# Another order of all queues, and another split of copies, casts, scalings and products among four engines, in a one-core attention and SoLU kernel

## The chip, the cores and the metric

The kernel runs on one core of one Trainium2 chip. A core has a matrix engine (PE, with its weight loads shown apart as PEld), a vector engine (DVE), an activation engine (ACT), a general engine (POOL), and a sync engine (SP) whose queue issues nearly all DMAs here. Each engine works through its own queue in order, and the queues wait for each other by semaphores. The metric is the device time of one execution in microseconds (us); lower is better.

## The reference

Clustered attention over 4 batches, 8 heads, 768 positions and head size 64, then a two-layer block with a softmax-gated activation (SoLU) and a normalisation, over 3072 tokens, 512 model features and 1024 hidden features:

```python
q_assign = np.argmax(np.einsum('bhsd,hcd->bhsc', q_n, c_n), axis=-1)
k_assign = np.argmax(np.einsum('bhsd,hcd->bhsc', k_n, c_n), axis=-1)
mask = q_assign[:, :, :, None] == k_assign[:, :, None, :]
scores = scale * np.matmul(q, k.transpose(0, 1, 3, 2))
scores = np.where(mask, scores, -1000000000.0)
attn = softmax(scores)
x = np.matmul(attn, v)            # heads side by side: (3072, 512)
h = x @ w_in
solu = h * softmax(h)
ln = (solu - mean(solu)) / np.sqrt(var(solu) + 1e-06) * g_ln
out = ln @ w_out
```

The softmax and mean lines are shortened here; they run along the last axis.

## The kernel before, in words

Every step is a small function that is registered under a name with its engine and with the names it must follow. A dictionary `AWAY` gives the engine of those steps that do not run on their usual one. A list `ORDER` names every step once; `run()` walks it and issues each step, so the list fixes the order of each engine's queue. Between queues only the data decide.

The names, with the lines that the profile shows:

- `ld`, `lv`, `lo`, `li`, `lc`, `lg`: loads of q and k, v, w_out, w_in, centroids and the norm's scale (SP's queue, two of them on ACT's). `tx`, `tu`: DMA transposes of attention output and of u. `ou`: output.
- Start of batch 0, pair of heads by pair: `tp` transposes q and k on PE (L396) into a PSUM bank, `xa`/`xt` copy the two halves out (L407 on ACT, L409 on DVE). From batch 1 on `xt` is one DVE transpose (L421). A pair's `ca` casts fill the operands `qbig` and `kbig` (L437 on ACT, L439 and L441 otherwise).
- `cz`, `cp`, `cb`: the centroids are normalised on DVE (L925 last), transposed on PE (L931) and spread on DVE (L934). `cl` multiplies with the centroids (L470). `tb`, `mx`, `oh`, `ot` turn that into one-hot rows on DVE (L479, L489, L493, L505 or L500). `pl` copies these below q and k (L529 on ACT, L531 otherwise), so that one product gives scores and mask. `bl` clears a part (L543).
- `S`: scores, 144 regions of 1024 columns in two halves `.0` and `.1` (L641). `E`: exponential of one region on ACT (L651). `V`: product with v (L663), v cast by `cv` (L554 on ACT, L556 otherwise). `N`: division by the sums on DVE (L675, L686). The scores use two PSUM tiles in turn: S of region n waits for E of region n-2.
- Tiles of 128 tokens, f = 0 to 23: `h` first product (L774), `hm` copy with running minimum on DVE (L784), `ex` exponential on ACT (L800), `u` the product h times e (L807, DVE or POOL), `bn`, `as`, `ag`, `al` the statistics (L818, L837, L823 and L825, L842), `y` second product (L846), `sc` scaling of the result (L859 on ACT, L861 on DVE).
- `me`, `mk`, `mf`, `km`, `ce`: w_out is centred once (L602, L611, L614, L618 or L622 and L624). `wi` casts w_in (L580). For the last two tiles u is transposed on PE (`ptu`, L761) and kept by `tu` (L768 DVE, L770 ACT).

Of the kernel before, what the change touches and what calls it, by code (L numbers as in the profile page):

```python
# [39 lines left out]
ld0.3.1 lg lv0.2 lo1 lo2 lo0 cx z5 cy cz wu tp0.0.0.0 tp0.0.0.1 tp0.0.1.0 tp0.0.1.1 cp xa0.0.0  # L40
xt0.0.0 xa0.0.1 xt0.0.1 tp0.1.0.0 xa0.1.0 cb cl0.0 tb0.0 mx0.0 oh0.0 ot0.0 ca0.0.0.0.0 z3
ca0.0.1.0.0 ca0.0.0.0.1 cc ca0.0.0.1.1 ca0.0.0.1.0 pl0.0.1.1 pl0.0.0.0 ca0.0.1.0.1 ca0.0.1.1.1
ca0.0.1.1.0 tp0.1.0.1 tp0.1.1.0 xt0.1.0 xa0.1.1 cl0.0.1 tp0.1.1.1 cv0.0.1 xt0.1.1 pl0.0.0.1
tp0.2.0.0 tp0.2.0.1 tb0.0.1 mx0.0.1 oh0.0.1 ot0.0.1 pl0.0.1.0.1 pl0.0.1.0.0 pl0.0.1.1.1 cl0.1 sg
pl0.0.1.1.0 z1 ca0.1.1.0 cv0.0.0 ca0.1.0.0 xa0.2.0 pl0.0.1.0 tp0.2.1.0 xt0.2.0 xa0.2.1 S0.0 S0.1
E0 tp0.2.1.1 xt0.2.1 S1.0 tp0.3.0.0 S1.1 S2.0 S2.1 tp0.3.0.1 tb0.1 mx0.1 oh0.1 xa0.3.0 E1 E2 cl0.2
xt0.3.0 S3.0 S3.1 V0.0 V0.1 V1.0 S4.0 S4.1 V1.1 tp0.3.1.0 tb0.2 E3 S5.0 S5.1 E4 E5 ot0.1 N0 mx0.2
gt tp0.3.1.1 S6.0 S6.1 V2.0 V2.1 S7.0 S7.1 V3.0 V3.1 xa0.3.1 gk xt0.3.1 cl0.3 E6 E7 cv0.1.0
pl0.1.1.1 ca0.1.0.1 ca0.3.0.0 pl0.1.1.0 ca0.3.0.1 z2 ca0.1.1.1 oh0.2 pl0.1.0.0 pl0.1.0.1 gw S8.0
S8.1 S9.0 S9.1 me0 me1 ot0.2 tb0.3 pl0.2.1.0 N1 pl0.2.0.0 mx0.3 mk oh0.3 ca0.2.0.0 ca0.2.1.0  # L50
ca0.3.1.0 ca0.2.1.1 pl0.2.1.1 pl0.2.0.1 E8 E9 ca0.2.0.1 S10.0 S10.1 S11.0 S11.1 V4.0 V4.1 V5.0
V5.1 E10 S12.0 S12.1 cv0.2.1 E11 E12 mf N2 ot0.3 pl0.3.0.0 ld1.0.0.0 li0 ld1.0.0.1 ld1.0.0.2
ld1.0.0 ld1.0.1.0 lv0.3 ld1.0.1.1 ld1.0.1.2 ld1.0.1 cv0.1.1 ca0.3.1.1 pl0.3.1.0 pl0.3.0.1 cv0.2.0
cv0.3.0 cv0.3.1 wi0 S13.0 S13.1 V6.0 V6.1 S14.0 S14.1 V7.0 V7.1 pl0.3.1.1 N3 km ce0 E13 E14 S15.0
S15.1 S16.0 S16.1 E15 E16 V8.0 V8.1 S17.0 S17.1 E17 V9.0 V9.1 S18.0 S18.1 E18 S19.0 S19.1 N4 ce5
V10.0 V10.1 V11.0 V11.1 S20.0 S20.1 E19 S21.0 S21.1 E20 E21 li1 li3 N5 V12.0 V12.1 ptx0 S22.0
S22.1 V13.0 V13.1 li2 xt1.0.0 xt1.0.1 tx0 xt1.1.0 xt1.1.1 ld1.2.0.0 ld1.2.0.1 ld1.2.0.2 ld1.2.0
ld1.2.1.0 ld1.2.1.1 ld1.2.1.2 ld1.2.1 S23.0 S23.1 cl1.0 E22 E23 S24.0 S24.1 E24 S25.0 S25.1 E25
ca1.0.0.1 cl1.1 N6 tb1.0 tb1.1 mx1.0 ce6 ce1 ca1.0.1.0 wi1 wi3 wi2 z4 ca1.1.0.0 ca1.0.1.1
ca1.1.1.0 ca1.0.0.0 S26.0 V14.0 V14.1 S26.1 S27.0 V15.0 S27.1 V15.1 h0.0.0 h0.0.1 N7 E26 E27 S28.0  # L60
S28.1 E28 V16.0 V16.1 V17.0 S29.0 S29.1 h0.1.0 V17.1 S30.0 S30.1 E29 E30 oh1.0 hm0.0 N8 ot1.0 ce2
pl1.0.1.0 pl1.0.0.1 pl1.0.1.1 bl1.0 ce3 lv1.0 tx2 lv1.1 lv1.2 ld2.0.0.0 ld2.0.0.1 ld2.0.0.2 h0.1.1
S31.0 S31.1 V18.0 V18.1 V19.0 S32.0 S32.1 V19.1 h1.0.0 N9 hm0.1 pl1.0.0.0 xt1.2.0 E31 S33.0 S33.1
E32 E33 h1.0.1 S34.0 S34.1 V20.0 V20.1 V21.0 S35.0 S35.1 V21.1 h1.1.0 E34 E35 S36.0 S36.1 N10
hm1.0 xt1.2.1 h1.1.1 S37.0 S37.1 V22.0 V22.1 V23.0 E36 E37 S38.0 S38.1 E38 V23.1 cl1.2 N11 tb1.2
ce4 hm1.1 ex0.0 cv1.0.0 cv1.0.1 u0.0 ca1.1.0.1 S39.0 S39.1 S40.0 S40.1 V24.0 V24.1 h2.0.0 h2.0.1
V25.0 xt1.3.0 E39 E40 ex1.0 h2.1.0 h2.1.1 S41.0 S41.1 S42.0 hm2.0 h3.0.0 S42.1 V25.1 xt1.3.1 hm2.1
V26.0 V26.1 h3.0.1 E41 cl1.3 S43.0 as0 bn0.0 N12 tb1.3 mx1.2 oh1.2 bn0.1 E42 S43.1 S44.0 S44.1
V27.0 ex2.0 E43 E44 V27.1 h3.1.0 h3.1.1 V28.0 S45.0 S45.1 S46.0 S46.1 V28.1 V29.0 E45 E46 tu0
V29.1 y0.0 S47.0 S47.1 y0.1 N13 cv1.1.0 ca1.2.0.0 u1.0 ca1.2.1.0 ca1.1.1.1 cv1.1.1 ca1.3.0.1 as1  # L70
ca1.2.0.1 bn1.0 hm3.0 ot1.2 ce7 S48.0 S48.1 y0.2 V30.0 E47 E48 S49.0 S49.1 E49 tx4 ld2.0.0
ld2.0.1.0 tu1 ld2.0.1.1 ld2.0.1.2 ld2.0.1 lv1.3 ld2.2.0.0 ld2.2.0.1 ld2.2.0.2 V30.1 V31.0 V31.1
S50.0 S50.1 h4.0.0 S51.0 S51.1 E50 E51 V32.0 V32.1 y0.3 S52.0 S52.1 bn1.1 hm3.1 ag0 N14 pl1.2.0.0
pl1.2.0.1 pl1.2.1.1 pl1.2.1.0 h4.0.1 as2 bl1.2 hm4.0 ag1 al0 u2.0 ca1.2.1.1 S53.0 S53.1 V33.0
V33.1 h4.1.0 xt2.0.0 sc0 h4.1.1 hm4.1 bn2.0 bn2.1 E52 E53 ex3.0 V34.0 S54.0 S54.1 S55.0 S55.1 E54
V34.1 V35.0 h5.0.0 h5.0.1 S56.0 S56.1 y1.0 E55 S57.0 S57.1 E56 cv1.2.0 V35.1 E57 y1.1 hm5.0 N15
tu2 ou0 ld2.2.0 ld2.2.1.0 ld2.2.1.1 y1.2 S58.0 S58.1 E58 h5.1.0 S59.0 S59.1 V36.0 V36.1 V37.0
V37.1 V38.0 S60.0 S60.1 h5.1.1 E59 E60 ex4.0 V38.1 y1.3 S61.0 S61.1 S62.0 S62.1 E61 E62 xt2.0.1
xt2.1.0 u3.0 ca2.0.0.1 ca2.0.0.0 al1 ag2 xt2.1.1 hm5.1 bn3.0 N16 bn3.1 cl2.1 cl2.0 tb2.1 ca1.3.1.0
cv1.2.1 ca1.3.0.0 as3 ag3 tb2.0 cv1.3.0 ca1.3.1.1 al2 u4.0 ca2.0.1.1 al3 ca2.1.0.0 ca2.1.1.0  # L80
cv1.3.1 V39.0 V39.1 S63.0 S63.1 S64.0 S64.1 V40.0 V40.1 sc1 V41.0 V41.1 y2.0 mx2.0 as4 N17 E63
S65.0 S65.1 E64 E65 y2.1 S66.0 S66.1 y2.2 y2.3 E66 tu3 tu4 ou1 ld2.2.1.2 ld2.2.1 S67.0 S67.1 V42.0
V42.1 S68.0 S68.1 V43.0 V43.1 sc2 oh2.0 ot2.0 N18 pl2.0.1.1 pl2.0.0.0 bn4.0 xt2.2.0 pl2.0.0.1
pl2.0.1.0 ca2.0.1.0 y3.0 E67 S69.0 S69.1 y3.1 ca2.2.0.1 bl2.0 E68 E69 S70.0 S70.1 E70 y3.2 V44.0
y3.3 V44.1 V45.0 S71.0 S71.1 S72.0 S72.1 V45.1 sc3 N19 tx6 y4.0 y4.1 E71 E72 S73.0 S73.1 E73 V46.0
V46.1 S74.0 S74.1 E74 y4.2 y4.3 V47.0 lv2.0 ou2 ld3.0.0.0 lv2.1 tx8 lv2.2 ex5.0 V47.1 S75.0 S75.1
E75 S76.0 h6.0.0 h6.0.1 S76.1 E76 bn4.1 xt2.2.1 ag4 xt2.3.0 N20 cv2.0.0 V48.0 V48.1 V49.0 h6.1.0
S77.0 S77.1 S78.0 S78.1 hm6.0 u5.0 bn5.0 V49.1 h6.1.1 hm6.1 V50.0 V50.1 cv2.0.1 xt2.3.1 N21
cv2.1.1 ca2.2.1.0 h7.0.0 h7.0.1 hm7.0 E77 E78 ca2.2.0.0 ca2.2.1.1 ca2.1.1.1 ca2.3.1.0 ex6.0 u6.0
cv2.1.0 ca2.3.0.0 al4 ca2.1.0.1 S79.0 S79.1 S80.0 S80.1 h7.1.0 E79 E80 V51.0 h7.1.1 V51.1 h8.0.0  # L90
S81.0 S81.1 h8.0.1 S82.0 S82.1 E81 E82 V52.0 V52.1 V53.0 V53.1 bn5.1 hm7.1 hm8.0 N22 cl2.3 cl2.2
tb2.3 tb2.2 mx2.2 sc4 oh2.2 ot2.2 pl2.2.0.0 S83.0 S83.1 S84.0 S84.1 V54.0 h8.1.0 h8.1.1 ex7.0 E83
S85.0 S85.1 E84 E85 pl2.2.0.1 pl2.2.1.1 V54.1 V55.0 V55.1 h9.0.0 ld3.0.0.1 ld3.0.0.2 tu5 S86.0
# [1267 lines left out]
```

## Time and profile before

| what | value |
|---|---|
| runs (us) | 222.46, 222.06, 220.9; median 222.06 |
| the profiled execution's own time | 221.02 us |
| its span, first to last instruction | 219.2 us |
| granted PE clock | 1.00 |
| DVE busy | 185.0 us (84%) |
| ACT busy | 193.0 us (88%) |
| POOL busy | 159.0 us (73%) |

A span of 219.2 us in an execution of 221.02 us leaves 1.8 us around it. "Busy" is the time in which at least one instruction of the engine is under way. A wait is put down to whatever ended it.

### The profile page before, as it was taken

Reading aid. Unit: us, or ns where it says so; the run is one execution under the profiler, and the core shown is the slowest. Engines: PE = TensorE matmul, PEld = TensorE weight load, DVE = VectorE, ACT = ScalarE, POOL = GpSimd, SP = SyncE. Lnnn points to the kernel's source line nnn. Section 1 sums busy time; section 2 is a strip of 40 time slices with the busy share of each in tenths; the row PEclk is TensorE's granted clock in tenths of the full one; section 3 lists DMA queues with packets and bytes.
Section 4 is the critical chain, followed back from the end, with each engine's and each line's share of the span. In section 5 each row is a group of like instructions: output and inputs, shape, how many; then the busy total and the mean of one; then the engine's idle time right before and its main releaser. Section 6 shows DMA issues by size and latency. Waiting matters only on the chain.

```text
span 219.2 us, 6308 instructions
## 1 busy us (share of the span) xinstructions
PE 211.8 (97%) x2429; PEld 148.0 (68%) x2429; DVE 185.0 (84%) x429; ACT 193.0 (88%) x246; POOL 159.0 (73%) x198
## 2 busy tenths in 40 slices
PE   7799999999999999999999999999999999999993
PEld 3467477677678776777677677666677766755552
DVE  3699978978999999896899999994888756889893
ACT  4699999999999998999999989999999888785472
POOL 4586969987898999549939987979969154555530
PEclk9999999999999999999999999999999999999999
DMA  6999999999799992998989973939484329695614
GB/s 198 372 403 299 180 182 301 150 155 274 134 189 175 164 185 45 174 250 174 190 211 173 180 155 63 178 96 215 133 162 101 93 48 171 138 151 132 185 60 156
DMA packets 120910, 38.33 MB, mean 175 GB/s; under 512 B 109992, under 2 KB 116400, under 8 KB 120880
## 3 DMA queue, kind: packets, MB, share of 16 engines
q1 hardware_dynamic: 120448, 37.40, 81.1%
q10 hardware_dynamic: 432, 0.52, 0.7%
...
## 4 chain that ended last, share of the span: by engine, by line
PE 74%; ACT 10%; DVE 9%; issue 2%; DMA 2%; POOL 0%; SPq 0%; DVEq 0%
PE sb L641 22%; PE hb L774 17%; PE mb L846 15%; PE ob L663 12%; ACT e L651 7%; PE hb L470 3%; DMA raw<-in_k_dram 2%; DVE w_st L784 2%; DVE xt L421 2%; DVE bs L818 2%; PE hb L846 2%; ACT xt L407 1%; PE hb L396 1%; DVE x L686 1%; ACT v L554 1%
## 5 line engine op out<-in xcount | busy, mean ns | idle before, releaser
L651 ACT ACTIVATE e<-sb 128x1024 bf16<-128x1024 f32 x144 | 139.8, 1023 | 8.7 <-PE sb L641 7.9
L641 PE MATMUL sb<-qbig,kbig 80*128 80x256 bf16 (+3 forms) x648 | 83.7, 261 | 1.1 <-ACT e L651 1.0
L641 PEld LDWEIGHTS <-kbig 80*128 80x128 bf16 (+1 forms) x648 | 62.9, 119 | 25.5 <-issue 8.8
L807 POOL TENSOR_TENSOR u<-e_sb,w_st 128x1024 bf16<-128x1024 bf16 x21 | 45.0, 2144 | 19.3 <-ACT e_sb L800 13.1
L663 PEld LDWEIGHTS <-e 128*128 128x128 bf16 x1152 | 48.6, 97 | 10.4 <-DVE x L686 0.6
L774 PE MATMUL hb<-w_in_sb,xT 128*128 128x512 bf16 x192 | 53.4, 379 | 0.0
L663 PE MATMUL ob<-v,e 128*128 128x65 bf16 x1140 | 51.4, 193 | 0.0
L846 PE MATMUL mb<-w_out_c,uT 128*128 128x512 bf16 x168 | 45.6, 379 | 0.4 <-DVE y L861 0.4
L818 DVE BATCH_NORM_STATS2 bs<-u 128x6 f32<-128x512 bf16 x48 | 31.9, 681 | 1.1 <-POOL u L807 1.1
L800 ACT ACTIVATE e_sb<-w_st,nmax 128x1024 bf16<-128x1024 f32 (+1 forms) x25 | 27.8, 1113 | 5.5 <-DVE w_st L784 4.1
L441 POOL TENSOR_SCALAR kbig<-xt 64x768 bf16<-64x768 f32 (+1 forms) x32 | 28.4, 890 | 2.3 <-DVE xt L409 0.7
L439 POOL CAST qbig<-xt 64x768 bf16<-64x768 f32 (+1 forms) x31 | 25.0, 807 | 5.9 <-PE ob L663 2.7
L842 POOL TENSOR_TENSOR alpha<-var,halves 128x1 f32<-128x1 f32 x24 | 15.4, 643 | 11.7 <-DVE var L825 11.0
L421 DVE STREAM_TRANSPOSE xt<-raw 128x768 f32<-128x768 f32 x24 | 22.5, 959 | 0.1
L846 PEld LDWEIGHTS <-uT 128*128 128x128 bf16 x176 | 15.1, 97 | 9.8 <-issue 0.5
L774 PEld LDWEIGHTS <-xT 128*128 128x128 bf16 x192 | 15.8, 98 | 8.3
L686 DVE TENSOR_TENSOR x<-ob,den 128x256 bf16<-128x256 f32 (+2 forms) x40 | 19.0, 474 | 1.4
L784 DVE TENSOR_SCALAR_CACHE_REDUCE w_st<-hb 128x512 f32<-128x512 f32 x24 | 16.3, 681 | 4.0 <-PE hb L774 3.9
L784 DVE TENSOR_SCALAR_CACHE_REDUCE w_st<-hb,nmax 128x512 f32<-128x512 f32 x24 | 17.8, 742 | 2.1 <-PE hb L774 1.5
L675 DVE RECIPROCAL den<-ob 128x4 f32<-128x4 f32 (+2 forms) x40 | 7.1, 179 | 10.7 <-PE ob L663 10.4
L556 POOL CAST v<-vf 128x384 bf16<-128x384 f32 x22 | 11.7, 542 | 4.2 <-DMA vf<-in_v_dram 3.6
L531 POOL COPY kbig<-oht 32x768 f32<-32x768 f32 (+2 forms) x14 | 9.9, 711 | 3.2 <-DVE oht L505 1.3
...
## 6 DMA issues: line engine op xcount, KB each, us to landing
...
```

The source lines that it names most:

```text
L421: nc.vector.transpose(xts[b, p, i][:], raw_of(b, p, i))
L439: (nc.vector if e == "DVE" else nc.gpsimd).tensor_copy(dst, src)
L441: (nc.vector if e == "DVE" else nc.gpsimd).tensor_scalar(dst, src, scalar1=inv_C, scalar2=1.0, op0=Alu.mult, op1=Alu.mult)
L641: nc.tensor.matmul(reg[:, c:c + wd], kb[u, pp, side_of(h), keys], qb[u, pp, side_of(h), su * P:su * P + wd])
L651: nc.scalar.activation(es[r][:, :w], src, Act.Exp, scale=exp_scale, bias=-exp_scale)
L663: nc.tensor.matmul(ops_of(group_of[n])[:, s, :VW], es[r][:, c0:c0 + P], v1[index[b, pair_of(h)] % R][:, side_of(h), kt, :VW], start=(kt == ...
L774: nc.tensor.matmul(hb[f2][:], xTs[f][:, dc, :], w_in_sb[:, dc, f2 * BANK:(f2 + 1) * BANK], start=(dc == 0), stop=(dc == n_dc - 1))
L784: nc.vector.tensor_scalar(ff[f, "h"][:, f2 * BANK:(f2 + 1) * BANK], hb[f2][:], scalar1=-1.0, scalar2=nmax[:, f2 - 1:f2] if f2 else 3.0e38, ...
L800: nc.scalar.activation(ff[f, "e"][:, cols(f, f2)], ff[f, "h"][:, cols(f, f2)], Act.Exp, bias=ff[f, "nmax"][:, n_ff2 - 1:], scale=-1.0, acc ...
L807: (nc.vector if e == "DVE" else nc.gpsimd).tensor_tensor(ff[f, "u"][:, cols(f, f2)], ff[f, "e"][:, cols(f, f2)], ff[f, "h"][:, cols(f, f2) ...
L818: nc.vector.bn_stats(ff[f, "bs"][:, f2, :], ff[f, "u"][:, f2 * BANK:(f2 + 1) * BANK])
L846: nc.tensor.matmul(y_of(f, x), ff[f, "uT"][:, fc, :], w_out_c[:, fc, parts_of(f, x)], start=(fc == 0), stop=(fc == n_fc - 1))
```

## The change

Only the two tables differ; every step's code is the same, and every step is still there. Since the tables are three lines shorter, each line number after is three lower.

`AWAY` moves these steps (the numbers are counts of steps):

| step | from, to |
|---|---|
| `cv` (cast of v) | 9 ACT to POOL, 1 POOL to DVE |
| `ca` (cast of q or k) | 5 ACT to POOL, 3 POOL to ACT, 2 POOL to DVE |
| `pl` (one-hot rows into place) | 12 DVE to POOL, 2 ACT to POOL, 2 POOL to ACT, 2 POOL to DVE, 1 ACT to DVE |
| `xa`, `xt` (copies out of PSUM) | 4 ACT to DVE, 1 DVE to ACT |
| `sc` (scaling of the result) | 6 ACT to DVE, 4 DVE to ACT |
| `u` (product) | u11, u12, u15, u16 POOL to DVE; u20 and the halves u23.0, u23.1 DVE to POOL |
| `as`, `ce`, `bl`, `mk` | `as` 7 POOL to DVE, 1 back; `ce` 2 POOL to DVE, 1 back; `bl` 2 POOL to DVE, 1 back; `mk` DVE to ACT |

```diff
 AWAY.update(dict.fromkeys("""
-    ca0.0.0.0.0 ca0.0.0.0.1 ca0.0.0.1.0 ca0.0.0.1.1 ce1 ce3 pl0.0.1.1 u0.0 u1.0 u10.0 u11.0
+    ca0.0.0.0.0 ca0.0.0.0.1 ca0.0.0.1.0 ca0.0.0.1.1 pl0.0.1.0.1 pl0.0.1.1.1 u0.0 u1.0 u10.0 u13.0
...
 ORDER = """
-lc ld0.0.0.0 ld0.0.1.0 ld0.0.0 ld0.0.1 ld0.1.0 ld0.1.1 lv0.0 ld0.2.0 ld0.2.1 ld0.3.0 lo3 lv0.1
+wu lc cx cy ld0.0.0.0 tp0.0.0.0 z2 ld0.0.1.0 ld0.0.0 tp0.0.0.1 xa0.0.0 tp0.0.1.0 ld0.0.1 cz xt0.0.0
```

`ORDER` is a new permutation of all names. On PE the scores S, E and V keep their sequence among themselves; what lies between them (transposes, cluster products, h and y) has moved.

The first place is the start. PE's queue before, from the third transpose of pair 0 (into `ob`) to the second cluster product:

```order
L396 MATMUL ob<-ident_f,raw 128x128 x3
L396 MATMUL sb_91<-ident_f,raw 128x128 x3
L931 MATMUL mb<-ident_f,fold 128x128
L396 MATMUL hb_92<-ident_f,raw 128x128 x3
L470 MATMUL mb<-xt,g_wide 32x192 x4
L396 MATMUL hb_93<-ident_f,raw 128x128 x3
L396 MATMUL hb_92<-ident_f,raw 128x128 x3
L470 MATMUL mb<-xt,g_wide 32x192 x4
```

PE's queue after, the same stretch:

```order
L393 MATMUL ob<-ident_f,raw 128x128 x3
L928 MATMUL mb<-ident_f,fold 128x128
L393 MATMUL sb_91<-ident_f,raw 128x128 x3
L467 MATMUL mb<-xt,g_wide 32x192 x4
L393 MATMUL hb_92<-ident_f,raw 128x128 x3
L393 MATMUL hb_93<-ident_f,raw 128x128 x3
L467 MATMUL mb<-xt,g_wide 32x192 x4
```

The centroids' transpose (into `mb` from `fold`) now stands ahead of the fourth transpose of pair 0, the first cluster product right behind it instead of one transpose later, and one transpose fewer stands ahead of the first score.

The second place is ACT's queue among the first exponentials; `e` is an exponential, the others are copies and casts. Before, from the seventh exponential on:

```order
L651 ACTIVATE e<-sb_90 128x1024
L651 ACTIVATE e<-sb_91 128x1024
L554 CAST v_1_103<-vf 128x6x64
L529 COPY kbig_99<-oht 32x384
L651 ACTIVATE e<-sb_90 128x1024
L651 ACTIVATE e<-sb_91 128x1024
L437 ACTIVATE qbig_97<-xt 64x6x128
L651 ACTIVATE e<-sb_90 128x1024
L554 CAST v_2_104<-vf 128x6x64
L651 ACTIVATE e<-sb_91 128x1024
```

After, from the tenth exponential to the fourteenth:

```order
L648 ACTIVATE e<-sb_91 128x1024
L648 ACTIVATE e<-sb_90 128x1024
L526 COPY qbig_97<-oht 32x384
L648 ACTIVATE e<-sb_91 128x1024
L648 ACTIVATE e<-sb_90 128x1024
L606 COPY y<-hb_93 128x512
L648 ACTIVATE e<-sb_91 128x1024
```

Between the seventh and the twelfth exponential before stand two casts of v, one placing and one cast of q; after, between the third and the fourteenth stand one placing and `mk`, and no other work until the first `ex`.

The third place is the end of POOL's queue: `u` are the products, `alpha` the powers that `sc` waits for. Before:

```order
L807 TENSOR_TENSOR u<-e_sb,w_st 128x1024
L837 TENSOR_SCALAR es_3820<-esum 128x1
L837 TENSOR_SCALAR es_3822<-esum 128x1
L842 TENSOR_TENSOR alpha<-var,halves 128x1
L807 TENSOR_TENSOR u<-e_sb,w_st 128x1024
L842 TENSOR_TENSOR alpha<-var,halves 128x1 x4
```

After:

```order
L804 TENSOR_TENSOR u<-e_sb,w_st 128x1024 x2
L839 TENSOR_TENSOR alpha<-var,halves 128x1
L804 TENSOR_TENSOR u<-e_sb,w_st 128x1024
L834 TENSOR_SCALAR es_3902<-esum 128x1
L839 TENSOR_TENSOR alpha<-var,halves 128x1
L804 TENSOR_TENSOR u<-e_sb,w_st 128x512 x2
L839 TENSOR_TENSOR alpha<-var,halves 128x1 x3
```

Before, u21 and u22 run here, with u20 and the two halves of u23 on DVE; after, u20 to u23 all run here one behind the other.

More of the change, by code (lines that the diff above doesn't have):

```diff
@@ L40 @@
[L40 to L93, printed above, removed]
@@ new lines @@
+ag16 bn17.0 S143.0 bn17.1 y14.1 as17 y14.2 y14.3 sc14 h20.1.0 S143.1 ou13 h20.1.1 ex18.0 as18 V94.1
+u18.0 hm20.0 ex19.0 y15.0 hm20.1 ag17 y15.1 y15.2 E143 ou14 y15.3 h21.0.0 al15 u19.0 h21.0.1 bn18.0
+tu17 sc15 V95.0 bn18.1 ex20.0 ou15 y16.0 al16 y16.1 tx22 y16.2 y16.3 hm21.0 h21.1.0 h21.1.1 N39
+ag18 sc16 V95.1 bn19.0 y17.0 y17.1 tu18 y17.2 hm21.1 as19 ou16 h22.0.0 y17.3 al17 ptx23.0 tu19 as20
+al18 sc17 bn19.1 h22.0.1 h22.1.0 y18.0 u20.0 ex21.0 y18.1 u21.0 y18.2 tx23.0 N40 y18.3 sc18 bn20.0
@@ new lines @@
+h22.1.1 hm22.0 h23.0.0 ag19 tu20 y19.0 y19.1 hm22.1 bn20.1 ptx23.1 bn21.0 ex22.0 y19.2 al19 ou17
+y19.3 tx23.1 h23.1.0 h23.0.1 h23.1.1 u22.0 sc19 bn21.1 hm23.0 hm23.1 tu21 y20.0 as21 ou19 ag20
+y20.1 ex23.0 y20.2 y20.3 ex23.1 ptu22.0 y21.0 al20 u23.0 y21.1 u23.1 ag21 tu22.0 bn22.0 sc20
+ptu22.1 bn22.1 y21.2 tu22.1 y21.3 y22.0 as22 al21 ag22 bn23.0 ptu23.0 y22.1 ptu23.1 y22.2 al22
+y22.3 ou18 tu23.0 as23 sc21 y23.0.0 sc22 bn23.1 y23.0.1 y23.1.0 tu23.1 ou21 ag23 al23 y23.0.2
+y23.0.3 ou20 sc23.0 y23.1.1 y23.1.2 ou22 y23.1.3 ou23.0 sc23.1 ou23.1
```

154 lines of the change are left out of this document (97 added, 57 removed).

## The prediction

> **What bounds the kernel now.** I read the stretches of the span first. Columns: us, busy time of PE, PEld, DVE, ACT and POOL with instruction counts, clock, DMA share, GB/s.
>
> ```profile
> 12.20:35.00 22.80, 21.70 (x281) 15.71 (x280) 19.70 (x44) 22.41 (x29) 17.97 (x30) 1.00 1.01 255
> 35.00:60.80 25.80, 25.80 (x340) 18.41 (x340) 23.42 (x48) 25.46 (x29) 22.46 (x25) 1.00 0.96 200
> 60.80:119.30 58.50, 58.15 (x716) 44.04 (x714) 53.48 (x111) 56.14 (x68) 47.09 (x51) 1.00 0.98 178
> 119.30:195.00 75.70, 75.70 (x896) 53.53 (x893) 62.37 (x153) 68.80 (x87) 53.84 (x59) 1.00 0.71 132
> 195.00:216.00 21.00, 20.86 (x149) 11.30 (x146) 18.99 (x54) 12.82 (x22) 11.22 (x13) 1.00 0.49 138
> sum 219.20, PE 211.76 PEld 148.01 DVE 184.98 ACT 193.03 POOL 159.03; mean PE 26.47 PEld 18.50 DVE 23.12 ACT 24.13 POOL 19.88
> ```
>
> From 35 us on PE leaves 0.35 + 0.14 = 0.5 us idle. PE's work is the same after the change, so from there an order can lose much and gain 0.5 us. Before that, PE waits: for the start, then for the exponentials; from 12.2 to 35 ACT is busy 22.41 of 22.80, more than PE. So I read the chain of waits (start, length, what), and who waited for whom (us in all, times, longest):
>
> ```profile
> 27.45 0.80 ACT e L651
> ...
> 33.79 1.09 ACT e L651
> ```
>
> ```profile
> ACT e L651 <- PE sb L641: 7.9, 18, 1.1
> ```
>
> Eight exponentials start from 27.45 to 33.79: 6.34/7 = 0.906 us each, ACT's pace. Until the first products h come in, that pace is the bound, and each thing beside an exponential in ACT's queue costs its length; on top come the 7.9 us in which ACT waited for a score.
>
> **The start.** The timeline (start, length, engine, line, instruction):
>
> ```profile
> 5.06 0.52 DVE L925 TENSOR_TENSOR fold<-c_all,c_inv 128x128 f32<-128x128 f32 x1
> 5.55 0.56 DVE L409 COPY xt<-ob 128x384 f32<-128x384 f32 x1
> 6.18 0.55 PE L396 MATMUL sb<-ident_f,raw 128*128 128x128 f32 x3 [0.67 <-DMA raw<-in_k_dram]
> 6.57 0.27 PE L931 MATMUL mb<-ident_f,fold 128*128 128x128 f32 x1
> 6.65 0.50 POOL L439 CAST qbig<-xt 64x384 bf16<-64x384 f32 x1
> 6.88 0.42 DVE L934 TENSOR_TENSOR g_wide<-mb,upper 128x256 f32<-128x256 f32 x1 [0.77 <-PE mb L931]
> 7.73 0.53 PE L470 MATMUL mb<-xt,g_wide 128*32 128x192 f32 x8
> 8.99 0.53 PE L470 MATMUL mb<-xt,g_wide 128*32 128x192 f32 x8
> 11.29 0.64 DVE L505 STREAM_TRANSPOSE oht<-oh 128x192 bf16<-128x192 bf16 x2
> 12.25 0.60 PE L641 MATMUL sb<-qbig,kbig 80*128 80x256 bf16 x4
> 12.42 0.34 POOL L531 COPY kbig<-oht 32x192 f32<-32x192 f32 x1
> 12.89 1.02 ACT L651 ACTIVATE e<-sb 128x1024 bf16<-128x1024 f32 x1
> ```
>
> Before, the centroids are ready at 5.58 but are transposed at 6.57, behind a transpose that waits for a load. After, they go first, about 5.7. DVE's copy (now `xt0.0.0`, 0.56) ends at 6.14 and `cb` (0.42) at 6.56, so the first cluster product follows the transpose of 6.18 directly, at 6.75 instead of 7.73. The second comes at about 7.95 instead of 8.99. The one-hot rows of pair 0, ready at 11.93, come 1.0 earlier, at 10.95. POOL's seven half casts, 0.46 from start to start (0.50 long), end at 9.5, and its first two placings (0.34 each) at 10.2; ACT's two end near 10.5. PE is then the last: with one transpose fewer ahead, the first score starts at 10.95, not 12.25. Term 1: **-1.3**. The second region needs POOL's next four placings: 10.95 + 4 x 0.34 = 12.3, then 0.6 to its exponential, 12.95. The loads keep their order up to pair 1; pair 2's q moves ahead of v, so no transpose here waits longer for DMA; w_out and w_in move behind, needed long after.
>
> **The exponentials.** What left ACT, the row of the starts before, and POOL's rows:
>
> ```profile
> L407 ACT COPY xt<-hb 128x384 f32<-128x384 f32 x11 | 5.2, 481 | 2.4 <-PE hb L396 2.3
> L554 ACT CAST v<-vf 128x384 bf16<-128x384 f32 x10 | 5.1, 511 | 0.1
> L437 ACT ACTIVATE qbig<-xt 64x768 bf16<-64x768 f32 x3 | 2.5, 842 | 0.1
> L529 ACT COPY kbig<-oht 32x384 f32<-32x384 f32 x1 | 0.5, 507 | 0.0
> 26.54 10.35 ACT L651 ACTIVATE e<-sb 128x1024 bf16<-128x1024 f32 x11
> 42.62 3.91 ACT L651 ACTIVATE e<-sb 128x1024 bf16<-128x1024 f32 x4
> L439 POOL CAST qbig<-xt 64x768 bf16<-64x768 f32 x27 | 23.0, 852 | 5.0 <-PE ob L663 2.7 <-PE sb L641 1.1 <-ACT xt L407 0.4
> L556 POOL CAST v<-vf 128x384 bf16<-128x384 f32 x22 | 11.7, 542 | 4.2 <-DMA vf<-in_v_dram 3.6
> ```
>
> The row of 26.54 begins with the twelfth exponential (E11), that of 42.62 with E27. Before, ACT does 2 copies, 2 casts of v, a placing and a cast of q between E0 and E11: 0.96 + 1.02 + 0.51 + 0.84 = 3.3; after, one cast of v and one placing, 1.0. From 11.6 (E0, 1.3 earlier): 11 x 0.906 + 1.0 = E11 at 22.6, if nothing is late. What is late next is POOL, which takes over casts and placings. Region 9 needs pair 1: from 10.95 four small placings (1.4), six casts (6 x 0.85), two casts of v (1.1), two placings and the spread centroids (0.5 each, as ACT's placing) end at 20.1, where ACT could take E9 at 20.3, and its score must start 0.6 before that. I count 0.85 for this and for PE's cluster product behind DVE's last copy: E11 at 23.45, 3.1 earlier. Then ACT has `mk` alone (an estimate: 0.48 for a copy of 384 columns makes 0.6 for 512), PE's `mf` behind it holds the next region back, 0.35 as I place it, and sixteen exponentials at 0.906 put E27 at 38.9, 3.7 earlier. Of this, two products h are only moved: before they stand ahead of region 28, after behind it.
>
> ```profile
> 41.96 0.86 PE hb L774 x4
> ```
>
> Net PE lead 3.7 - 0.86 = 2.8, of which 1.5 is **term 2**. From 0 (POOL or DVE eats it) to -2.35 (no lateness).
>
> **The middle, 40 to 195 us.** The same products on a full PE: 0, no better than -0.5 (its idle above). Casts of v and placings on POOL come before their readers by as much as before; `u` on DVE for f = 11, 12, 15, 16 takes 1.22 instead of 2.14 (next fence), off the path, as y stands much further behind its h than before. Loads on SP: a new order, but the scores run earlier, so `tx6`, `tx12` and `tx22` come close to their h. Before, PE never waits for one, so their price lies between 0 and D's below; I take 0.
>
> ```profile
> 199.41 1.22 DVE L807 TENSOR_TENSOR u<-e_sb,w_st 128x1024 bf16<-128x1024 bf16 x1
> 199.57 1.46 POOL L842 TENSOR_TENSOR alpha<-var,halves 128x1 f32<-128x1 f32 x1 [2.51 <-DVE var L825]
> 203.99 0.55 POOL L842 TENSOR_TENSOR alpha<-var,halves 128x1 f32<-128x1 f32 x1 [0.30 <-DVE var L825]
> 206.27 2.14 POOL L807 TENSOR_TENSOR u<-e_sb,w_st 128x1024 bf16<-128x1024 bf16 x1 [1.74 <-issue]
> L493 DVE TENSOR_TENSOR oh<-cst,mx x11: 359/948/1553, 9.1 to 146.9; 128x768 bf16<-128x768 f32 x6, 128x384 bf16<-128x384 f32 x3, 128x192 bf16<-128x192 f32 x2
> ```
>
> A power that starts inside a DVE product takes 1.46, not 0.55: the product holds POOL up by 0.91. Three more full products on DVE hold it up by 2.7 in all, against four POOL products of 2.14 that it no longer has: free for the path, and 2.7 if POOL were the path there. The Trainium skill, page "SBUF — State Buffer", section "Who interferes with whom", says that a DVE instruction with two SBUF inputs contends with a POOL instruction that reads SBUF, and that the later of the two is blocked wholly until the other ends. The trace agrees (1.46 against 0.55). By it each hold could last the full 1.22, or 3.7 in all, also off the path.
>
> **The tail.** The last u goes from DVE to POOL:
>
> ```profile
> 207.72 1.89 PE L846 MATMUL mb<-w_out_c,uT 128*128 128x512 bf16 x8
> 209.31 0.72 ACT L800 ACTIVATE e_sb<-w_st,nmax 128x512 bf16<-128x512 f32 x1 [2.30 <-DVE w_st L784]
> 210.22 1.34 DVE L807 TENSOR_TENSOR u<-e_sb,w_st 128x512 bf16<-128x512 bf16 x2
> 212.48 0.61 PE L761 MATMUL sb<-ident_b,u 128*128 128x128 bf16 x8
> ```
>
> The halves end at 211.56 and PE takes them from 212.48: 0.9 of cover. On POOL they take half of 2.14 each, 0.8 more in all. After, the first half of `ex23` ends 2.3 behind h23 (210.03 against 207.72); the power of tile 20 stands ahead on POOL and delays by 0.3; two halves end at 4.8. PE has 20 products of y (0.215 each, a quarter of the 0.86 above) and three transposes of 0.22 before it takes the second half: 5.0. With cover the cost is 0, without it 0.8; I take **+0.3**.
>
> Sum: -1.3 - 1.5 + 0.3 = **-2.5**. Span 219.2 to 216.7. The profiled execution's 221.02 becomes 218.5; it lies 1.04 below the median 222.06, from which the sum gives 219.6. I forecast 219.0, between the two.
>
> **Rivals.**
> (B) POOL is the gate from the first regions on: it must do 3.3 us more by region 12 than before. For it: the 20.1 against 20.3 above, and holds by DVE (0.91 each). Against: POOL idles 4.8 of 22.8 there. Then term 2 falls to 0 or -0.5: -1.0 to -1.5 in all, 220.3 on the same middle ground (221.54).
> (C) Slower: DVE becomes the bound between regions 44 and 92. Before, this stretch is 60.8 to 119.3, with DVE busy 53.5 of 58.5. After, its queue there holds 3 more `bn`, 2 more `N` and `xt` each, one `tb`, `mx`, `oh`, `hm` more and 2 `pl` fewer, 12 instructions net at a mean of 53.5/111 = 0.48 or, since the long ones come in, up to 0.58: 6 to 7. PE's work there shrinks by 1.3 (7 steps of y less, 2 of h more at 0.43, a cluster product more). DVE would need 59.5 to 60.5 in PE's 56.8: 2.7 to 3.7 lost, and up to 1.5 more where three `oh` meet a POOL cast (1.55 against the median 0.95). That is +0.2 to +2.7, I take +1.5: 223.0. It decides once DVE is over 98% busy there while PE shows gaps. Against: DVE's lengths overlap, and it has since the start less behind it.
> (D) Nothing to measure: PE is full from 35 us, and the early lead is lost to late h tiles or loads; 221.5.
>
> **How the numbers follow.** Chances: forecast 0.55, B 0.25, C 0.12, D 0.08. The range holds the forecast's low end (-1.3 - 2.35 - 0.5 = -4.2 at 221.0, 216.8) and reaches through B and D to C's lower half: 222.6. Over 1% (2.2 us, about what this kernel's runs can tell from no change) means under 219.84: most of the forecast (0.50) and a little of B (0.03) make faster 0.53; the rest of the forecast, most of B and D (0.05 + 0.21 + 0.06) make same 0.32; C, with ends of B and D, makes slower 0.15.
>
> **What would show it.** Term 1: first score near 11.0, first exponential near 11.6. Term 2: E11 near 23.5, E27 near 39, exponentials 0.91 apart between; B would show PE waiting for POOL's L528 or L436 there. The tail: PE idle before its last transposes of u. Wrong if PE's idle time after 40 us exceeds 2 us; the waits would name DVE (C), a DMA into `xT`, or POOL.

## The result, and the profile after

The changed kernel is slower: 230.31 us (median of four runs, 229.53 to 231.92) against 221.48 (220.72 to 222.46); the ratio is 1.0397, with a 95% interval of 1.0350 to 1.0443. The profiled execution took 231.05, its span is 229.3. The forecast was 219.0, in a range that ended at 222.6. One execution of a later version took 436.3 us, and two of the kernel before that ran beside it 362.3 and 226.3; no comparison below uses them.

Where the 10.1 us of span lie can be read from PE, whose work is the same. I take the start of a score in the trace and subtract the lengths of all that stands ahead of it in PE's queue (0.217 for half a score, 0.181 for half a product with v, 0.43 for a product h or y, 0.72 for a cluster product, and so on: the tenth percentile of each kind's start-to-start time in the trace of before). What is left is called PE's loss: time in which it waited or ran slowly. The end of the span is treated alike (205.5 us of work).

| PE's loss up to the score of region | before | after | more than before |
|---|---|---|---|
| 0 | 4.0 | 4.9 | 0.9 |
| 24 | 7.8 | 9.1 | 1.3 |
| 28 | 8.2 | 10.7 | 2.5 |
| 44 | 8.7 | 11.1 | 2.4 |
| 48 | 8.9 | 16.0 | 7.1 |
| 143 | 11.5 | 20.9 | 9.4 |
| end | 13.7 | 23.8 | 10.1 |

So nearly half, 4.7, arises in one place, between regions 44 and 48. The line of busy times of the profile's page and the longest of PE's waits after (us in all, times, longest):

```profile
PE 216.8 (95%) x2397; PEld 149.5 (65%) x2429; DVE 195.0 (85%) x436; ACT 186.8 (81%) x230; POOL 158.9 (69%) x206
```

```profile
PE ob L660 <- DVE x L683: 3.2, 2, 2.8
```

ACT has 6.2 us less to do and DVE 10 more: part of that is work, and part is waiting inside instructions, as the timelines of DVE, POOL and PE at this place show (start, length, instruction):

```profile
61.73 4.83 DVE L615 SCALAR_TENSOR_TENSOR w_out_c<-w_g,g_ln,y 128x512 bf16<-128x512 f32 x1
66.49 0.18 DVE L672 RECIPROCAL den<-ob 128x6 f32<-128x6 f32 x1
66.71 0.56 DVE L683 TENSOR_TENSOR x<-ob,den 128x384 bf16<-128x384 f32 x1
```

```profile
60.52 2.14 POOL L804 TENSOR_TENSOR u<-e_sb,w_st 128x1024 bf16<-128x1024 bf16 x1
62.62 0.49 POOL L553 CAST v<-vf 128x384 bf16<-128x384 f32 x1
63.09 0.82 POOL L438 TENSOR_SCALAR kbig<-xt 64x768 bf16<-64x768 f32 x1
63.89 2.13 POOL L804 TENSOR_TENSOR u<-e_sb,w_st 128x1024 bf16<-128x1024 bf16 x1
```

```profile
67.32 1.40 PE L660 MATMUL ob<-v,e 128*128 128x65 bf16 x24 [2.85 <-DVE x L683]
```

`ce1`, a product that takes 0.74 elsewhere, begins while POOL is in `u0` and ends 0.5 after POOL has finished `u1`: 4.1 us of it are waiting. The change moved this step from POOL to DVE and put it just ahead of the division `N12`, for which PE's next product with v waits. The stretches of 2 us show what that costs beyond the gap (columns as in the prediction; the last but two is the clock):

```profile
64.00:66.00 2.00, 0.48 (x4) 0.13 (x2) 2.00 (x1) 1.06 (x2) 2.00 (x2) 1.00 0.64 122
66.00:68.00 2.00, 0.68 (x15) 0.68 (x16) 1.93 (x5) 0.12 (x1) 2.00 (x4) 0.87 0.40 80
68.00:70.00 2.00, 2.00 (x30) 1.75 (x28) 2.00 (x4) 0.90 (x2) 0.18 (x1) 0.50 1.08 175
70.00:72.00 2.00, 1.78 (x15) 1.23 (x14) 1.89 (x5) 1.43 (x2) 0.00 (x0) 0.77 0.49 78
```

After the gap PE's clock is granted at half: a mean of 0.87, 0.50 and 0.77 over 2 us each is 0.5 + 2.0 + 0.9 = 3.4 us at half speed, or 1.7 lost. With the 2.85 of waiting that makes 4.55 of the 4.7 in the table.

### The profile page after: what moved, and what is told of

It reads as the page before. It is cut to its first block, busy times and chain, and to the rows that moved or that the text cites. A ratio compares the mean times of both kernels' runs of the same rounds, so it can differ in the third digit from the quotient of the medians.

```text
span 229.3 us, 6268 instructions
## 1 busy us (share of the span) xinstructions
PE 216.8 (95%) x2397; PEld 149.5 (65%) x2429; DVE 195.0 (85%) x436; ACT 186.8 (81%) x230; POOL 158.9 (69%) x206
## 4 chain that ended last, share of the span: by engine, by line
PE 83%; DVE 11%; issue 2%; DMA 2%; ACT 1%; ACTq 0%; DVEq 0%
PE sb L638 25%; PE hb L771 17%; PE mb L843 16%; PE ob L660 14%; DVE w_out_c L615 4%; PE hb L467 4%; DMA raw<-in_q_dram 2%; PE hb L843 2%; PE hb L393 1%; DVE xt L406 1%; PE mb L467 1%; DVE oht L502 1%; PE hb L599 1%; DVE x L683 1%; DVE xt L418 1%
## 5 line engine op out<-in xcount | busy, mean ns | idle before, releaser
L638 PE MATMUL sb<-qbig,kbig 80*128 80x256 bf16 (+3 forms) x648 | 93.7, 263 | 1.7 <-DVE kbig L540 0.6
L660 PEld LDWEIGHTS <-e 128*128 128x128 bf16 x1152 | 52.3, 98 | 16.7 <-DVE x L683 3.6
L660 PE MATMUL ob<-v,e 128*128 128x65 bf16 x1140 | 56.6, 195 | 3.4 <-DVE x L683 3.2
L804 POOL TENSOR_TENSOR u<-e_sb,w_st 128x1024 bf16<-128x1024 bf16 (+1 forms) x20 | 40.8, 2045 | 18.7 <-ACT e_sb L797 14.7
L771 PE MATMUL hb<-w_in_sb,xT 128*128 128x512 bf16 x170 | 50.4, 381 | 0.7
L843 PE MATMUL mb<-w_out_c,uT 128*128 128x512 bf16 x158 | 42.7, 379 | 0.7 <-DVE y L858 0.2
L839 POOL TENSOR_TENSOR alpha<-var,halves 128x1 f32<-128x1 f32 x24 | 13.3, 555 | 20.7 <-DVE var L822 20.4
L528 POOL COPY kbig<-oht 32x768 f32<-32x768 f32 (+2 forms) x18 | 13.9, 771 | 8.9 <-DVE oht L497 6.3
L553 POOL CAST v<-vf 128x384 bf16<-128x384 f32 x30 | 15.8, 531 | 0.7
L856 ACT ACTIVATE y<-mb,alpha 128x512 f32<-128x512 f32 x10 | 6.9, 687 | 8.5 <-PE mb L843 4.9
```

The costliest lines, as they stand in the source:

```text
L638: nc.tensor.matmul(reg[:, c:c + wd], kb[u, pp, side_of(h), keys], qb[u, pp, side_of(h), su * P:su * P + wd])
L660: nc.tensor.matmul(ops_of(group_of[n])[:, s, :VW], es[r][:, c0:c0 + P], v1[index[b, pair_of(h)] % R][:, side_of(h), kt, :VW], start=(kt == ...
L771: nc.tensor.matmul(hb[f2][:], xTs[f][:, dc, :], w_in_sb[:, dc, f2 * BANK:(f2 + 1) * BANK], start=(dc == 0), stop=(dc == n_dc - 1))
L804: (nc.vector if e == "DVE" else nc.gpsimd).tensor_tensor(ff[f, "u"][:, cols(f, f2)], ff[f, "e"][:, cols(f, f2)], ff[f, "h"][:, cols(f, f2) ...
L843: nc.tensor.matmul(y_of(f, x), ff[f, "uT"][:, fc, :], w_out_c[:, fc, parts_of(f, x)], start=(fc == 0), stop=(fc == n_fc - 1))
```

## The experiments

All numbers of PE's loss are from each run's own trace. The kernel before ran beside them, at medians of 221.1 to 221.5. In diffs of the order a line is a name.

**ce1 ahead of POOL's products.**

```diff
 ce2
+ce1
...
-ce1
 cl1.3
```

> The changed kernel, with one step moved in the order: ce1 (the centring product of a quarter of w_out, on DVE) stands right behind ce2, some 10 us earlier, before POOL's first product u. Theory: in the changed kernel ce1 was held for 4.1 us by POOL's reads (4.83 against 0.74 for ce2), the division N12 behind it kept PE idle for 2.85 us, and PE then ran at half clock for about 3.4 us, which costs 1.7 more. Then ce1 takes 0.7 to 1.3, no idle time of PE over 0.6 remains between 60 and 72, no granted clock under 1 there, and the time falls by 4.0 to 5.0, from 230.3 to about 225.8. Rival: DVE has too much to do there (9.5 us of each 10), and N12 is late whatever stands ahead: PE still idles over 1.5 us for a division and the time stays over 228.5.

Measured: 225.8 us (224.01 to 227.31), ratio 1.0205 (1.0132 to 1.0279), 4.5 less than the changed kernel. The six products of this kind on DVE (shortest, median and longest in ns) in the changed kernel, and with `ce1` early:

```profile
L615 DVE SCALAR_TENSOR_TENSOR w_out_c<-w_g,g_ln,y x6: 743/1270/4833, 33.8 to 61.7; 128x512 bf16<-128x512 f32 x6
```

```profile
L618 DVE SCALAR_TENSOR_TENSOR w_out_c<-w_g,g_ln,y x6: 709/746/1245, 31.9 to 49.3; 128x512 bf16<-128x512 f32 x6
```

PE's loss between regions 44 and 48 is 0.26 instead of 4.84, and the clock stays at 1.00. DVE was not too full there.

**u1 behind other casts.** `u1` was moved behind two casts of v and one of k; `ce1` stayed.

> The changed kernel, with POOL's second product u1 moved behind the next two casts of v and one cast of k; ce1 stays where it is on DVE and still begins during u0. It tells by what ce1 is held. If only by the two-input products u, it ends about 0.6 after u0, after 1.6 us instead of 4.83, and the time falls to about 226. If any POOL instruction that reads SBUF and follows without a gap keeps it waiting, it still takes 4 us or more, and the time stays near 230. Rival without a hold: the length of 4.83 has another cause (a late operand), and it stays 4.83 wherever u1 stands.

Measured: 228.79 us. Neither alone. DVE's row, and POOL's at the moment of release:

```profile
60.33 4.42 DVE L618 SCALAR_TENSOR_TENSOR w_out_c<-w_g,g_ln,y 128x512 bf16<-128x512 f32 x1
```

```profile
63.38 0.83 POOL L441 TENSOR_SCALAR kbig<-xt 64x768 bf16<-64x768 f32 x1
64.18 2.57 POOL L807 TENSOR_TENSOR u<-e_sb,w_st 128x1024 bf16<-128x1024 bf16 x1
```

So plain casts hold `ce1` as well; here it got in ahead of `u1`, which then took 2.57 instead of 2.14. PE waited 2.4 us for `N12`, without a drop of the clock in this execution (0.996 on the mean of the span). The other three of this kernel have 0.985 to 0.991, which points to one there: 3.4 us at half clock take 0.007 off the mean.

**ce1 and ce2 exchanged** (one execution).

```diff
-ce2
+ce1
...
-ce1
+ce2
```

> The changed kernel with ce1 and ce2 exchanged in the order: ce1 runs at 51.6, ce2 at 61.8 while POOL works through u0, a cast, a cast and u1. Theory: the place decides, so ce2 now takes over 4 us and ce1 0.7 to 1.3, and the time stays at 229 to 231. Rival: ce1 has an operand that is late or badly placed; then ce2 takes under 1.8 us there and the time falls to about 226.

Measured: 231.4 us, and the other step is now the long one, at the same place:

```profile
61.99 4.83 DVE L618 SCALAR_TENSOR_TENSOR w_out_c<-w_g,g_ln,y 128x512 bf16<-128x512 f32 x1
```

The place decides, not the operand.

**POOL quiet behind u0** (one execution). `cv1.0.1` went ahead of `u0.0`; the cast of k, `u1`, `tu1` and the next casts went behind `pl1.2.1.1`.

> The changed kernel with POOL left quiet while ce1 runs: v's cast stands ahead of u0, and behind u0 POOL's next step is a placing that waits for the one-hot rows behind ce1; the cast of k, u1 and the other casts follow that. ce1 stays at its place on DVE and begins during u0. Theory: what held ce1 was POOL's chain of reads without a break; with none behind u0 it ends about 0.6 after u0 and takes 1.2 to 1.8 us instead of 4.83, and the division N12 behind it no longer keeps PE idle over 0.6 us. POOL's own casts come 5 us later, so the whole time may stand anywhere from 225 to 229. Rival: ce1 is held by something else (the DMA transpose of u0, or a late operand); then it takes 4 us or more here too.

Measured: 231.51 us. DVE's and POOL's rows:

```profile
59.96 2.33 DVE L618 SCALAR_TENSOR_TENSOR w_out_c<-w_g,g_ln,y 128x512 bf16<-128x512 f32 x1
...
68.87 3.52 DVE L531 COPY qbig<-oht 32x768 f32<-32x768 f32 x1
```

```profile
59.60 2.15 POOL L807 TENSOR_TENSOR u<-e_sb,w_st 128x1024 bf16<-128x1024 bf16 x1
...
68.59 0.83 POOL L441 TENSOR_SCALAR kbig<-xt 64x768 bf16<-64x768 f32 x1
69.39 2.14 POOL L807 TENSOR_TENSOR u<-e_sb,w_st 128x1024 bf16<-128x1024 bf16 x1
```

With nothing behind `u0`, `ce1` ends 0.5 after it and takes 2.33, 0.5 more than I gave only because it began earlier in `u0`; PE has no wait for `N12`. That settles what held it: POOL's instructions one behind the other. The time is no better, since the chain now comes 5 us later and meets the next DVE step, a copy of 0.79 that takes 3.52, until `u1` ends again. PE then waits elsewhere:

```profile
76.69 0.67 PE L663 MATMUL ob<-v,e 128*128 128x65 bf16 x12 [2.93 <-POOL v L556]
```

Behind this wait the clock is halved again, for 3.4 us.

**ce1 behind the division** (one execution).

```diff
-ce1
 cl1.3
...
 N12
+ce1
```

> The changed kernel with ce1 one place later on DVE, behind the division N12 instead of ahead of it. Theory: ce1 is held as before (it begins at about 62.6, still ahead of u1's end at 66, and takes 2 to 4.5 us), but N12 is on time, so PE's wait of 2.85 us for N12 goes; what waits next are the cluster's maximum and the division N13, which PE needs some 3 us later, so that PE idles 0 to 1.5 us there. The time lies between 225.8 (nothing lost) and 228.5. Rival: the held product costs the same wherever it stands on DVE, since everything behind it is late: PE idles over 2.5 us for N13 or for a tile of h, and the time stays over 229.

Measured: 227.99 us. DVE's rows, and the row of PE with the longest wait there (in brackets):

```profile
60.88 0.56 DVE L686 TENSOR_TENSOR x<-ob,den 128x384 bf16<-128x384 f32 x1
61.36 4.03 DVE L618 SCALAR_TENSOR_TENSOR w_out_c<-w_g,g_ln,y 128x512 bf16<-128x512 f32 x1
```

```profile
65.94 0.38 PE L774 MATMUL hb<-w_in_sb,xT 128*128 128x512 bf16 x1 [1.11 <-DVE cst L479]
```

The hold is the same, but what stands behind it is needed later: PE loses 1.5 up to region 48 and 3.1 up to region 56 (0.8 with `ce1` early, 5.0 in the changed kernel), and the clock isn't cut. In this execution nearly half of the damage (1.9 of 4.2 us) goes with the place ahead of `N12`.

**The early part as before.** Order and engines of before up to region 28, of the changed kernel behind.

> Spliced: order and engines of the kernel before up to the scores of region 28 (there ce1 is still on POOL), those of the changed kernel for all that is left. By the starts of the scores, less PE's own work ahead of them, the changed kernel loses 2.6 us more than before up to region 28, 4.7 around ce1, and 2.9 behind that. Theory: the three are apart, so region 28 starts as before (42.8), and the time is 230.3 - 2.6 - 4.7 = 223.0, still above 221.5. Rival: the loss behind region 28 comes from the early lateness or from the clock, and the time is 221.5 or less; or it is a full DVE in the middle that loses it again, and the time stays over 226.

Measured: 227.63 us: missed. At the seam PE waits for a placing that POOL reaches late, and loses 3.2 us up to region 36:

```profile
PE sb L642 <- POOL kbig L532: 2.1, 1, 2.1
```

What it does tell: from region 52 to 143 it loses 5.1 us, as does the kernel with `ce1` early (5.2); the kernel before loses 2.6. That loss doesn't come from the early part.

**The late part as before.** Up to region 51 the kernel with `ce1` early, behind it that of before.

> Spliced: the order and engines of the kernel with ce1 early up to region 51, those of the kernel before from region 52 on. By the starts of the scores less PE's own work, the kernel with ce1 early had lost 8.75 us up to region 52, the kernel before 8.98; from there to the end the one loses 8.0 and the other 4.7. Theory: the loss behind region 52 belongs to the changed order of that part (cluster products one by one between bf16 products, late divisions, the tail). Then the span is 219 to 220, the time 220.7 to 221.7, level with the kernel before. Rival: the early order leaves DVE or POOL behind, and the late part loses 2 us or more here as well: over 223.

Measured: 222.89 us, ratio 1.0046 (1.0003 to 1.0089). PE loses 1.8 us between regions 52 and 68 (before 0.8), where the two orders meet, and from there to region 143 1.73, exactly as before (4.2 with `ce1` early). The median lies above the 220.7 to 221.7 of the theory and just under the rival's 223: the later loss belongs to the changed order and engines of that part, but the seam costs 1.0 of what was to be gained. That later loss is of several pieces, each read from the traces of before and of `ce1` early and not tried alone, except the first: 0.78 at region 127 (next run); 0.16 to 0.21 for each cluster product that stands alone on PE between bf16 products, 1.38 in eight places against 0.55 in four where two stand together; the rest in pieces of up to 0.44.

**bl3.2 back on POOL, u23 back on DVE.**

> The kernel with ce1 early, and two more moves of engine undone: the clearing of kbig bl3.2 back on POOL, and the two halves of u23 back on DVE. Theory: in the run with ce1 early PE waits 0.59 for bl3.2 before the scores of region 127 (POOL idles 6 us there), which goes; and the last products y wait 0.59 for the last copy of the transposed u, because u23 on POOL is 0.8 later, which shrinks to under 0.2. Together 1.0 to 1.2 less: 224.7 against 225.8. Rival for the tail: the copy is late by its place in the order, not by u23's engine; then the wait of 0.6 stays and the gain is 0.6 to 0.7.

Measured: 224.3 us (223.66 to 224.59). With `ce1` early, `bl3.2` on DVE keeps PE, while POOL is idle:

```profile
160.40 0.70 DVE L543 MEMSET kbig<- 16x768 f32 x1 [0.21 <-issue]
```

```profile
161.24 0.29 PE L641 MATMUL sb<-qbig,kbig 80*128 80x128 bf16 x2 [0.59 <-DVE kbig L543]
```

On POOL the loss between regions 124 and 128 falls from 0.86 to 0.09. The half on `u23` was wrong, and further than the rival said: on DVE the last wait grows to 1.08, since DVE's statistics are now later. From region 143's score to the end of the span it takes 29.8 us instead of 29.35, so the lower time isn't the work of this half.

```profile
218.23 0.61 PE L845 MATMUL ob<-w_out_c,w_g 128*128 128x256 bf16 x4 [1.08 <-DVE w_g L767]
```

**tu23.1 ahead of y23.1.0** (on top of `ce1` early and `bl3.2` on POOL).

```diff
+tu23.1
 y23.1.0
-tu23.1
```

> The kernel with ce1 early, the clearing bl3.2 back on POOL (u23 stays on POOL), and the last copy of the transposed u, tu23.1 on DVE, ahead of the first last-tile product y23.1.0 in the order instead of behind it; both use the same PSUM tile. Theory: with ce1 early alone, DVE stood idle for 1.28 us ahead of that copy although the transposes had ended 1.6 us before, because y23.1.0 was issued first and writes into the tile that the copy reads; PE then waited 0.59 for the copy. Now the copy starts at once, PE's wait of 0.59 goes, and the stretch from the scores of region 143 to the end takes 0.5 to 0.6 less than with ce1 early alone; with bl3.2's 0.78 the time is about 1.3 under that kernel's, near 223.7 to 224.5. Rival: the copy is held by the balance of DVE's statistics, then the wait stays at 0.5 or more, as in the run with u23 on DVE (1.08).

With `ce1` early the copy and PE read:

```profile
217.28 0.42 DVE L768 COPY w_g<-sb 128x512 bf16<-128x512 bf16 x1 [1.28 <-PE sb L846]
```

```profile
217.76 0.61 PE L846 MATMUL ob<-w_out_c,w_g 128*128 128x256 bf16 x4 [0.59 <-DVE w_g L768]
```

With the copy ahead neither row has a wait, and from region 143's score to PE's end it takes 25.25 us instead of 26.15. But the span then ends 3.8 us after PE instead of 3.2, in this execution and in those of the three versions built on it, so that 0.3 is left of the 0.9. Why the end behind PE is longer isn't shown. The time is 224.34 (223.81 to 224.67), the same as in the run before it, which had `bl3.2` right as well. So the wait is explained, its worth in the time isn't shown.

**The exponentials: cc later, then cl0.3 later.** First the spreading of the centroids on POOL goes behind the placings of pair 1, then on PE the last cluster product of batch 0 behind region 9's scores.

> As the kernel before it (ce1 early, bl3.2 on POOL, tu23.1 ahead of y23.1.0), and on POOL the spreading of the centroids cc (0.73) stands behind the two placings of pair 1 instead of ahead of them. It tests whether POOL gates the exponentials at region 9, as the second forecast named. Theory: the score of region 9 waits 0.6 for POOL; now that wait goes, the tenth exponential comes 0.5 to 0.7 earlier after the first one, and region 28 0.3 to 0.6 earlier, and the time falls by 0.3 to 0.6. Rival: DVE, 9.6 of 10 us busy there, holds the next regions back; then region 12 to 16 are no earlier and the time stays within 0.2 of the kernel before it.

> As the kernel with cc later, and on PE the last cluster product of batch 0 (cl0.3) stands behind the scores of region 9 instead of ahead of them, with the step of w_out's sums that follows it on POOL (gw) behind it. In the kernel before it, region 9 waited on PE behind cl0.3, whose second half waited 0.5 for a copy on DVE; from the first exponential to the tenth it took 10.2 us, to the seventeenth 19.0 (in the kernel before the change 10.4 and 18.2). Theory: this queue order is what ate the exponentials' gain; then the tenth comes 0.6 to 0.9 earlier after the first (9.4 to 9.6), the seventeenth 0.5 to 0.9 earlier (18.1 to 18.5). Rival: DVE's one-hot rows and copies for pairs 2 and 3, which come one by one on a DVE that is 96% busy, set regions 10 to 16; then the tenth is earlier, but the seventeenth is not, 18.8 to 19.1.

Measured: 224.21 and 224.12 us. ACT's exponentials, with `cc` later (E8 is the last of the first row, E9 the second row):

```profile
18.04 3.84 ACT L650 ACTIVATE e<-sb 128x1024 bf16<-128x1024 f32 x4
22.67 1.02 ACT L650 ACTIVATE e<-sb 128x1024 bf16<-128x1024 f32 x1 [0.78 <-PE sb L640]
```

and with `cl0.3` later as well (E9 is the last of the first row):

```profile
17.19 4.79 ACT L650 ACTIVATE e<-sb 128x1024 bf16<-128x1024 f32 x5
22.89 1.02 ACT L650 ACTIVATE e<-sb 128x1024 bf16<-128x1024 f32 x1 [0.91 <-PE sb L640]
```

`cc` changes nothing: E9 comes 10.24 after E0 with and without it. `cl0.3` does: 9.39. But the gap comes back at E10 (the second row, 0.91): E10 stands 11.3 behind E0 (11.5 without the edit), E11 13.7 (13.2), and E16 19.1 (18.97; 18.2 in the kernel before). These are the numbers of the second rival, but its cause isn't shown. Between the scores of regions 9 and 10 now stands the moved `cl0.3` itself, and ahead of region 11's scores PE waits for `gw`, the step on POOL that was moved along with it:

```profile
23.61 1.06 PE L601 MATMUL hb<-w_g,g_wide 128*32 128x512 f32 x8 [0.63 <-POOL g_wide L591]
```

DVE works without a gap there, two casts of k moved from POOL among its steps, yet no wait of PE's products in that stretch is put down to DVE.

**ce3 back on POOL** (on top of all these).

> As the kernel with cl0.3 later, and ce3 back on POOL as before the change. In four of the executions seen so far of the changed order (ce1 early, and three built on it) DVE's products ce7 and ce3 met no cast of w_in on POOL, and PE lost 0.5 us between regions 24 and 28; in the others both were held (1.52 and 1.29 instead of 0.71) and it lost 1.6. Theory: with ce3 off DVE at most ce7 is held, the division N6 is on time, and PE loses 0.5 to 1.0 between regions 24 and 28 whenever the casts come; the time is up to 0.7 lower than that of the kernel with cl0.3 later. Rival: ce3's 2.05 us on POOL delay the casts of q and k there as much, and the loss stays at 1.3 or more.

> The same kernel as in the run with ce3 on POOL, whose profiled execution was a disturbed one of 434.6 us and tells nothing. Expected as there: with ce3 off DVE, PE loses 0.5 to 1.0 us between the scores of regions 24 and 28 whenever w_in's casts come (1.6 in the executions in which ce7 and ce3 were both held). Rival: ce3's 2.05 us on POOL delay the casts of q and k as much, and the loss stays at 1.3 or more.

The first run's executions give 223.82 to 224.75 us, the second run 224.41. With `ce3` on DVE (the kernel with `cl0.3` later), and with it on POOL:

```profile
L617 DVE SCALAR_TENSOR_TENSOR w_out_c<-w_g,g_ln,y x6: 741/998/1523, 32.4 to 50.8; 128x512 bf16<-128x512 f32 x6
```

```profile
L617 DVE SCALAR_TENSOR_TENSOR w_out_c<-w_g,g_ln,y x5: 743/748/1526, 33.1 to 50.7; 128x512 bf16<-128x512 f32 x5
```

`ce7` is still held (1.53), but PE loses 0.51 between regions 24 and 28 instead of 1.36 with `ce3` on DVE, and 1.66 in five other executions in which `ce7` and `ce3` were both held. Where neither was held, with `ce3` on DVE, it is 0.51 as well. So the gain of 0.85 is in that stretch, but the time shows none of it (224.41 against 224.12). In the two traces it is gone again by region 44: the first score came 0.75 later, and 0.4 is lost between regions 36 and 44.

**The centroids' transpose alone**, in the kernel before.

> The kernel before with the first piece of the change alone: the centroids' transpose cp ahead of the fourth transpose of pair 0, and the first cluster product right behind that. In the changed kernel the transposes up to 9.5 us took 0.85 to 0.90 instead of 0.50 to 0.55, as if PE had half its clock, and the first score came at 12.8 instead of the 10.95 foreseen. If that was a matter of when the loads land in that execution, here the first cluster product starts at 6.8 to 7.2 (before 7.73), the first score near 11.5 (before 12.25), and the time falls by 0.3 to 0.7. Rival: with cp early PE is slow until 9.5 here too, the first score is not before 12.2, and the time is 221.5 or up to 1 us more.

Measured: 221.34 us, ratio 1.0012 (0.9990 to 1.0034). The first score came at 12.96, although PE was at full speed from its fourth transpose on: the second half of q landed late.

```profile
PE hb L397 <- DMA raw<-in_q_dram: 1.6, 3, 1.0
```

So neither theory fits that execution, and alone the step is worth nothing that can be measured.

No version was faster than the kernel before.

## Why the prediction was wrong, point by point

**Term 1, the start (-1.3; measured +0.5).** The step that failed is that the transposes would take 0.55, as in the execution before. PE after, and with `ce1` early, whose start is the same:

```profile
4.85 0.90 PE L393 MATMUL hb<-ident_f,raw 128*128 128x128 f32 x3 [0.61 <-DMA raw<-in_q_dram]
...
7.32 0.87 PE L467 MATMUL mb<-xt,g_wide 128*32 128x192 f32 x8
...
9.55 0.53 PE L467 MATMUL mb<-xt,g_wide 128*32 128x192 f32 x8
```

```profile
5.85 0.55 PE L396 MATMUL sb<-ident_f,raw 128*128 128x128 f32 x3
...
10.92 0.60 PE L641 MATMUL sb<-qbig,kbig 80*128 80x256 bf16 x4
```

The order was read rightly: with PE at full speed early the first score comes at 10.92 (10.95 foreseen). But in the profiled execution after, PE runs slowly up to 9.5. A load that landed 0.4 later than before adds to it, but isn't the cause alone: with the centroids' transpose moved alone that load was later still (5.27 against 4.85) and PE was fast behind it. The trace's record of the granted clock begins with full speed at 9.46 after, at 4.90 before and at 4.14 with `ce1` early, each time when the transposes become short. In twelve profiled executions with the start after, this moment lies between 4.1 and 10.6 and the first score between 10.92 and 13.59, with a median of 11.6; the two executions that got full speed last (9.46 and 10.56) have the two latest first scores (12.78 and 13.59). With the start of before there are two, 12.25 and 12.03. So the term is about -0.5, with 2.7 us of scatter, and what sets the moment in one execution stays open.

**Term 2, the exponentials (-1.5; measured +1.7 from region 0 to 28).** That ACT would lose work was right; that the lateness would be 0.85 was the failing step. From E0 to E11 I gave 11.0 and 0.85, measured 13.2 (before 13.65); from E0 to E27 27.3, measured 30.1 (before 29.7). At E9 it is 10.2 instead of 8.7: on PE region 9 stands behind `cl0.3`, whose second half waits for a copy on DVE. I named that product and put too little on it. With it out of the way E9 came at 9.4, but the gain was gone at E11, where PE waited for POOL's `gw`; what would set the pace without that stays open. I read what left ACT and counted POOL's queue step by step, and DVE's, 19.70 of 22.80 us busy before in the row I had quoted, only in passing. The last 1.2 us, between regions 24 and 28, come with `ce7` held by POOL's cast of w_in and `ce3` by the cast of q behind it: the moves of `ce` weren't priced at all.

**The middle (0; measured 4.7 at regions 44 to 48, and 2.3 behind).** The failing step is that a lock between DVE and POOL is "off the path". I had the row (1.46 instead of 0.55) and looked at it from one side: POOL held by DVE's `u`. The other side, a DVE step held by POOL with a division behind it, decides, and it came through a step of 0.75 us that stood in my list of moves. The size was out of reach of the row too: the longest hold of a product on DVE in the trace before was 0.6 (`oh`, 1.55 against 0.95). The other part of the 4.7, 1.7 by the halved clock behind the wait, had no term at all.

**The tail (+0.3; measured +0.7).** Right in sign by luck, wrong in cause: not `u23`'s engine, but that the new order issues `y23.1.0` ahead of the copy out of the PSUM tile into which it writes; before, the copy stood first.

**The rivals.** C came nearest: DVE, between regions 44 and 92, and slower; but I priced it as load (98% busy, +0.2 to +2.7). With `ce1` early DVE has the same work, and PE loses 0.26 between regions 44 and 48 and 2.9 from 44 to 92 (7.1 after, 1.5 before). B was not shown: moving a step of POOL (`cc`) away from region 9 changed nothing. The sign for "wrong" did its work: after 40 us PE waits 4.6 us for DVE alone.

Of the 10.1 us of span, the profiled executions put 0.9 on the start, 1.2 on `ce7` and `ce3` held, 4.7 on `ce1`, 0.8 on `bl3.2`, 0.8 on the lone cluster products and 0.7 on the tail; the other 1.0 lies in smaller pieces. Only the step with `ce1` shows clearly in the times (4.5 of the 8.8 us between the medians). With `ce1` and `bl3.2` undone the kernel is still 3 us behind the one before, and with the last copy, `cc`, `cl0.3` and `ce3` changed as well it still is (224.41 against 221.34).
